# A searched instruction plan with two load queues and some operations free to go to either of two engines, for attention and two gated layers on one Trainium2 core

## The chip, the cores and the metric

The kernel runs on one core of one Trainium2 chip. A core has five instruction queues that run side by side, each in its own order: PE (matrix products), DVE (vector work), ACT (activations, copies), POOL (vector work, slower) and SP (here it only issues DMAs). They wait for each other by semaphores. The metric is device time in microseconds (us) of one launch, lower is better. Before the change three runs gave 1077.69, 1081.61 and 1084.92 us, with a median of 1081.61 us.

## The reference, cut to what matters

```python
scores = scale * np.matmul(q, k.transpose(0, 1, 3, 2))          # q, k, v: (4, 8, 576, 64)
thresh = np.max(scores, axis=-1, keepdims=True) - tau
scores = np.where(scores >= thresh, scores, -1000000000.0)
attn = np.exp(scores - np.max(scores, axis=-1, keepdims=True))
attn = attn / (np.sum(attn, axis=-1, keepdims=True) + 1e-09)
x = np.matmul(attn, v)                                           # then to (2304, 512)
h = x @ moe_w_in                                                 # (512, 2048)
x = (h * np.clip(h + 3.0, 0.0, 6.0) / 6.0) @ moe_w_out           # (2048, 512)
h = x @ moe2_w_in
out = (h * (1.0 / (1.0 + np.exp(-1.702 * h)))) @ moe2_w_out
```

## The kernel before, in words

A matrix product in full precision is done as three products of a high and a low part of each operand (high x high, high x low, low x high). Much of the work of DVE, ACT and POOL is making such parts: a copy to the reduced type gives the high part, a subtraction the low part.

The work has three stages. In **attention** a unit is one pair of heads of one batch (16 units). For each of its nine tiles PE makes scores (tile `ps`, L566; L582 and L598 in the first four units), DVE takes the row maximum (`nm`, L614) and the threshold (`th`, L615), ACT the exponential (`e`, L616), DVE cuts and sums it (L617). Then `e` is normalised (L630 on POOL, later units), transposed (PE L668 and ACT L671, or DVE and a DMA through memory), multiplied with v (L709, L726), and its result `xr` is split into `xh` and `xl`. Between the units of attention the **first half of the first gated layer** runs as its inputs come (`moe_a`: hidden products L785, gate L796 and L797, high part on ACT, low part on POOL, output products L805). Then come the rest of the first layer (`moe_b`) and the **second layer** (`moe2`, hidden products L942 by a scheme with fewer products, output products L805). Weights come as 64-bit numbers and are decoded in `decode` (ACT L419, DVE L420 to L422, POOL adds through the helper at L369) and split. The helpers at L366 (ACT copy) and L369 (two-operand operation on DVE or POOL) stand for many operations, so a row of theirs is told by its tiles.

Nothing of the order is written out by hand. Every operation is an entry of a plan with an engine, a cost in ns and dependencies. `settle` simulates the plan, ranks operations by how late they may run, then disturbs the ranks with nine fixed seeds (`KICKS`), ranks again after each, and the last simulated start times give the program's order on every queue. `PORT` names the operations of DVE and POOL that the plan doesn't let run at the same time. `fill` puts stand-in matmuls (L1105, of constants, their result unused) where the plan has PE idle for over about half a microsecond and a result bank is free. So a stand-in marks a gap that the plan itself sees:

```python
count = int((s - t) / 450 if s < 12000 else (s - t - 300) / 216)
if count > 0:
```

All DMAs are issued by SP, in plan order, and an SP wait holds back the issues behind it. For the first units, the two heads' k come in two loads of 64 rows (L526), their q in five (L525 and L530).

## Time and profile before

| | |
|---|---|
| median of three runs | 1081.61 us |
| the profiled execution | 1084.38 us |
| its span, first to last instruction | 1082.5 us |
| PE busy | 1057.6 us (98%) |
| DVE busy | 733.3 us (68%) |
| ACT busy | 634.3 us (59%) |
| POOL busy | 516.2 us (48%) |
| data moved | 141.78 MB, 131 GB/s on average |

Busy time is the union of an engine's instructions. The span is split below into six stretches: the start (0 to 24 us), the rest of the first units (to 62, where the first hidden product of the gated layer starts), the next units (to 135), attention with the first half of the first layer (to 433), the rest of the first layer (to 690), and the second layer (to the end).

### The profile page before, as it was taken

Reading aid. Unit: us, or ns where it says so; the run is one execution under the profiler, and the core shown is the slowest. Engines: PE = TensorE matmul, PEld = TensorE weight load, DVE = VectorE, ACT = ScalarE, POOL = GpSimd, SP = SyncE. Lnnn points to the kernel's source line nnn. Section 1 sums busy time; section 2 is a strip of 40 time slices with the busy share of each in tenths; the row PEclk is TensorE's granted clock in tenths of the full one; section 3 lists DMA queues with packets and bytes.
Section 4 is the critical chain, followed back from the end, with each engine's and each line's share of the span. In section 5 each row is a group of like instructions: output and inputs, shape, how many; then the busy total and the mean of one; then the engine's idle time right before and its main releaser. Section 6 shows DMA issues by size and latency. Waiting matters only on the chain.

```text
span 1082.5 us, 20424 instructions
## 1 busy us (share of the span) xinstructions
PE 1057.6 (98%) x7498; PEld 961.9 (89%) x7498; DVE 733.3 (68%) x1541; ACT 634.3 (59%) x1272; POOL 516.2 (48%) x597
## 2 busy tenths in 40 slices
PE   8899899999999999999999999999999999999998
PEld 6677788799889988999999999889988889989888
DVE  6898977777767772677874333888786684563634
ACT  4798777576657664766453234665565565444433
POOL 3688978776777662755474225432322333001000
PEclk9999999999999999999999999999999999999999
DMA  6334375655465435445744112426553542312202
GB/s 198 120 115 140 115 207 148 183 146 155 139 186 146 149 102 168 130 146 175 215 139 135 59 58 60 158 63 207 182 176 106 166 158 87 117 54 65 93 1 74
DMA packets 87172, 141.78 MB, mean 131 GB/s; under 512 B 8608, under 2 KB 51232, under 8 KB 85536
## 3 DMA queue, kind: packets, MB, share of 16 engines
q1 hardware_dynamic: 87072, 140.48, 43.0%
q8 instruction: 59, 0.97, 0.4%
q14 instruction: 41, 0.34, 0.1%
HBM read 97.32 MB, written 43.12 MB: 130 GB/s over the span
## 4 chain that ended last, share of the span: by engine, by line
PE 77%; DMA 8%; DVE 5%; POOL 3%; ACT 2%; SPq 2%; issue 2%; DVEq 0%; POOLq 0%; ACTq 0%
PE py L805 25%; PE pm L942 15%; PE pm L785 15%; PE pm L805 7%; PE pm L726 6%; PE ps L566 5%; PE pm L668 3%; DMA qk<-in_q_dram 1%; DMA kept<-wmstg 1%; DMA et<-turned 1%; DMA wrawstg<-in_w1i_dram 1%; POOL wmstg L369 1%; DMA yc<-ypd 1%; DMA wrawstg<-in_w1o_dram 1%; DVE nm L614 1%
## 5 line engine op out<-in xcount | busy, mean ns | idle before, releaser
L805 PE MATMUL py<-g,outhring 128*128 128x512 f32 (+2 forms) x1152 | 289.2, 338 | 6.1 <-DVE g L369 1.9
L805 PEld LDWEIGHTS py<-g,outhring 128*128 128x128 f32 x1152 | 193.5, 188 | 25.4 <-DVE g L369 4.3
L805 PE MATMUL py<-g,outlring 128*128 128x512 f32 (+2 forms) x576 | 193.4, 336 | 0.0
L785 PE MATMUL pm<-xh,inhring 128*128 128x256 f32 (+1 forms) x512 | 153.2, 299 | 0.2
L785 PE MATMUL pm<-xl,inhring 128*128 128x256 f32 (+1 forms) x512 | 150.8, 295 | 0.0
L785 PE MATMUL pm<-xh,inlring 128*128 128x256 f32 (+1 forms) x512 | 150.8, 294 | 0.0
L942 PE MATMUL pm<-outhring,inhring 128*128 128x256 f32 x512 | 144.7, 283 | 1.8 <-DVE c L369 1.5
L942 PE MATMUL pm<-outlring,inhring 128*128 128x256 f32 x512 | 143.9, 281 | 0.1
L942 PE MATMUL pm<-outhring,inlring 128*128 128x256 f32 x512 | 143.6, 281 | 0.0
L614 DVE TENSOR_REDUCE nm<-ps 128x1 f32<-128x576 f32 x144 | 106.8, 751 | 33.2 <-PE ps L566 27.3
L369 POOL TENSOR_TENSOR g<-t,g 128x256 fp32r<-128x256 f32 (+1 forms) x104 | 87.9, 850 | 78.6 <-ACT g L366 69.8
L617 DVE SCALAR_TENSOR_TENSOR e<-ps,th,e 128x576 f32<-128x576 f32 x128 | 102.4, 811 | 23.6 <-ACT e L616 22.6
L805 PEld LDWEIGHTS py<-g,outlring 128*128 128x128 f32 x576 | 108.2, 188 | 9.9
L369 POOL TENSOR_TENSOR wmstg<-wmstg,wrstg 128x512 uint32<-128x512 uint32 x48 | 66.2, 1380 | 103.6 <-DVE wmstg L422 67.8
L616 ACT ACTIVATE e<-ps,nm 128x576 f32<-128x576 f32 x128 | 93.2, 740 | 33.8 <-DVE nm L614 26.2
L796 ACT ACTIVATE t<-pm,half 128x256 f32<-128x256 f32 (+1 forms) x128 | 63.9, 499 | 77.8 <-PE pm L785 69.2
L805 PE MATMUL pm<-g,outhring 128*128 128x256 f32 (+1 forms) x512 | 108.1, 302 | 0.5 <-ACT et L671 0.5
L369 POOL TENSOR_TENSOR g<-tc,g 128x512 fp32r<-128x512 f32 x24 | 32.4, 1351 | 157.5 <-ACT g L366 135.8
L797 DVE SCALAR_TENSOR_TENSOR t<-t,pm 128x256 f32<-128x256 f32 (+1 forms) x128 | 57.4, 449 | 69.2 <-ACT t L796 66.3
L942 PEld LDWEIGHTS pm<-outhring,inhring 128*128 128x128 f32 x512 | 96.9, 189 | 6.0 <-DVE c L369 2.0
L942 PEld LDWEIGHTS pm<-outlring,inhring 128*128 128x128 f32 x512 | 96.9, 189 | 3.1 <-DVE outlring L369 0.3
L785 PEld LDWEIGHTS pm<-xh,inhring 128*128 128x128 f32 x512 | 96.6, 189 | 1.2 <-PE pm L1105 0.7
(114 smaller groups left out, 2428.7 us busy)
## 6 DMA issues: line engine op xcount, KB each, us to landing
turned<-tr SPq DMA_DIRECT2D x12, 1024.0 KB, 3.9
et<-turned SPq DMA_DIRECT2D x48, 256.0 KB, 6.0
wrawstg<-in_w1i_dram SPq DMA_DIRECT2D x16, 512.0 KB, 4.0
wrawstg<-in_w1o_dram SPq DMA_DIRECT2D x16, 512.0 KB, 3.9
wrawstg<-in_w2i_dram SPq DMA_DIRECT2D x16, 512.0 KB, 4.3
wrawstg<-in_w2o_dram SPq DMA_DIRECT2D x16, 512.0 KB, 4.1
qk<-in_k_dram SPq DMA_DIRECT2D x24, 288.0 KB, 3.8
qk<-in_q_dram SPq DMA_DIRECT2D x24, 288.0 KB, 3.6
```

Of the source, the lines that this page charges most:

```text
L369: return lambda: (nc.vector if eng == DVE else nc.gpsimd).tensor_tensor(out=o(), in0=a(), in1=b(), op=op)
L566: nc.tensor.matmul(ps.t[:, i, :SH], qss[hd].t[:, q0:q0 + P], w[hd].t[:, i * SH:(i + 1) * SH], start=a, stop=z)
L614: add(DVE, 665, K("R", s), "R", lambda: nc.vector.tensor_reduce(out=nm.t[:, c], in_=ps.t[:, :, :SH], op=ALU.max, axis=AX.XY, negate=True), ...
L616: add(ACT, 624, K("X", s), "X", lambda: nc.scalar.activation(out=ev(), in_=ps.t[:, :, :SH], func=ACTF.Exp, bias=nm.t[:, c]), [ps, (nm, s)] ...
L617: add(DVE, 729, K("M", s), "M", lambda: nc.vector.scalar_tensor_tensor(out=ev(), in0=ps.t[:, :, :SH], scalar=th.t[:, c], in1=ev(), op0=ALU ...
L668: nc.tensor.transpose(pt.t[:kn, o:o + P], e_of[s].t[:, keys(k)], id_b.t)
L726: nc.tensor.matmul(pv[p].t[64 * hd:64 * hd + 64, :CH[p][1]], v_(k, hd), x, start=k == 0, stop=k == 4)
L785: nc.tensor.matmul(ph.t[:, :n], a, v, start=(cc == 0 and i == 0), stop=(cc == KC - 1 and i == 2))
L796: add(ACT, 93 + act(n), K("RL"), "RL", lambda: nc.scalar.activation(out=tt_(), in_=pt(), func=ACTF.Relu, scale=1.0 / 6.0, bias=half_b.t), ...
L797: add(DVE, dve(n), K("GT"), "GT", lambda: nc.vector.scalar_tensor_tensor(out=tt_(), in0=tt_(), scalar=1.0, in1=pt(), op0=ALU.min, op1=ALU. ...
L805: nc.tensor.matmul(py.t[:, :n], a, v, start=(st and i == 0), stop=(sp and i == 2))
L942: nc.tensor.matmul(o.t[:, :n], u.t[:, ws], v.t[:, xv], start=(st and kk == 0 and i == 0), stop=(sp and kk == 1 and i == 2), skip_group_che ...
```

## The change

The plan's costs are nearer to some durations (decode on ACT 575 ns for 520, weight loads 1.4 times as long, POOL's two-operand work a little longer). The nine seeds become 28, and about 330 further steps (`SHAKES`) follow, each of which shifts the ranks in a small window; a negative number instead swaps one operation to its other engine. Operations that may swap have an `alt`: most splits (ACT to DVE, POOL to DVE and back), the normalisation (POOL to DVE), thresholds (DVE to ACT), the first step of decode (DVE to POOL), copies out of PE's banks (ACT to DVE). `tau` and the first half of the first q are issued by ACT; k of the first four units comes in one load of 128 rows.

```diff
-PORT = {DVE: {"W", "XHB", "XLB", "XD", "XLC", "GT2", "GL"}, POOL: {...}}
+PORT = {DVE: {"W", "XHB", "XLB", "XD", "XLC", "GT2", "GL", "qs", "N", "kl", "XL", "XH", "GH", "kh", "qh", "ql"}, POOL: {...}}
-KICKS = (9, 22, 44, 100, 235, 395, 771, 940, 4389)
+KICKS = (
+    1032833269, 966046151, -163, 557497160, -877, 57522857, 697246556, 315576823, 472954259, -947, 719353647, 1052280090, 511556057, 211244978, -5437, 720474978,
...
+SHAKES = (
+    584305649, -943, 243327645, 788971575, 33716921, 162258981, -1247, 1025097930, -949, 1049297085, 494265569, 331174672, -197, 382340551, 170708664, 94164452,
...
         for seed in KICKS:
-            self.order(kicked(key, length, seed))
-            key = self.latest()
+            if seed < 0:
+                op = self.ops[-seed]
+                (op.eng, op.cost, op.fn), op.alt = op.alt, (op.eng, op.cost, op.fn)
+                self.link()
+                key = self.latest()
+            else:
+                self.order(kicked(key, length, seed, kinds, len(names)))
+                key = self.latest()
             length = self.order(key)
+        ref = key
+        for seed in SHAKES:
+            if seed < 0:
+                op = self.ops[-seed]
+                (op.eng, op.cost, op.fn), op.alt = op.alt, (op.eng, op.cost, op.fn)
+            else:
+                key = kicked(key, length, seed, kinds, len(names), ref)
+        self.link()
+        self.order(key)
...
-    move(-30000, "tau", 4 * P, lambda: nc.sync.dma_start(out=tau_b.t, in_=tau), [], [tau_b])
+    move(-30000, "tau", 4 * P, lambda: nc.scalar.dma_start(out=tau_b.t, in_=tau), [], [tau_b], ACT)
...
-                move(K("ld"), "ldk", 256 * S, lambda r=r, h=2 * j + hd: nc.sync.dma_start(out=f32(khb.t)[r, :S], in_=k2[b, h, :64]), [], [(khb, hd)])
...
+                eng, q = (ACT, nc.scalar) if u + hd == 0 else (SP, nc.sync)
...
+            move(K("ld") - 8000 * (u == 0), "ldk", 512 * S * 1.4, lambda rows=rows: nc.sync.dma_start(out=f32(khb.t)[:, :S], in_=k2.rearrange("b h p s -> (b h p) s")[rows:rows + P]), [], [khb])
...
-            add(ACT, act(size), K("EH", at), "EH", lambda: nc.scalar.activation(out=dst(kn)[0], in_=dst(kn)[1](pt.t[:kn, :size]), func=ACTF.Copy), [pt], [(et, tag)])
+            add(ACT, act(size), K("EH", at), "EH", lambda: nc.scalar.activation(out=dst(kn)[0], in_=dst(kn)[1](pt.t[:kn, :size]), func=ACTF.Copy), [pt], [(et, tag)], (),
+                (DVE, dve(size), lambda: nc.vector.tensor_copy(out=dst(kn)[0], in_=dst(kn)[1](pt.t[:kn, :size]))))
```

What the swaps come to, counted from the two programs: 28 operations go from POOL to DVE (21 subtractions of two operands, 7 scalings), 33 from ACT to DVE (21 between buffers, 12 out of PE's banks), 11 scalings from DVE to POOL, 22 thresholds from DVE to ACT. PE's program has the same matmuls, but 31 stand-ins in 7 places in the place of 49 in 16: behind the first hidden product one is left where 19 stood. The rows of both programs at three places follow.

SP at the program's start, before (`g` holds q, `kqv` holds k, `wrawstg` the first raw weights):

```order
L381 DMA tau_106<-in_tau_dram 128x1
L525 DMA g_141<-in_q2_dram 64x256 x2
L526 DMA kqv_157<-in_k2_dram 64x576 x2
L525 DMA g_147<-in_q2_dram 64x256 x2
L526 DMA kqv_170<-in_k2_dram 64x576 x2
L382 DMA id_103<-in_ident_dram 128x128
L525 DMA g_151<-in_q2_dram 64x256 x2
L526 DMA kqv_175<-in_k2_dram 64x576 x2
L525 DMA g_155<-in_q2_dram 64x256 x2
L526 DMA kqv_181<-in_k2_dram 64x576 x2
L409 DMA wrawstg_244<-in_w1i_dram 128x4x256
```

SP at the same place now:

```order
L590 DMA g_140<-in_q2_dram 64x256
L592 DMA kqv_151<-in_k2_dram 128x576
L590 DMA g_148<-in_q2_dram 64x256 x2
L592 DMA kqv_168<-in_k2_dram 128x576
L444 DMA id_103<-in_ident_dram 128x128
L590 DMA g_154<-in_q2_dram 64x256
L592 DMA kqv_176<-in_k2_dram 128x576
L590 DMA g_154<-in_q2_dram 64x256
L590 DMA g_158<-in_q2_dram 64x256
L592 DMA kqv_184<-in_k2_dram 128x576
L590 DMA g_158<-in_q2_dram 64x256
L471 DMA wrawstg_224<-in_w1i_dram 128x4x256
```

The first weight load is the 19th issue before and the 13th now; the first k moves from the fourth and fifth issue to the second, and one q and `tau` stand on ACT's queue ahead of its table load.

DVE where the first weights are decoded, before (`wmstg` is the decoded tile, `nm`, `th` and `e` belong to score tiles):

```order
L617 SCALAR_TENSOR_TENSOR e_247,sm_221<-ps_233,th_213,e_247 128x576
L615 TENSOR_SCALAR th_213<-nm_210,nt_108 128x1
L617 SCALAR_TENSOR_TENSOR e_255,sm_221<-ps_241,th_213,e_255 128x576
L614 TENSOR_REDUCE nm_282<-ps_268 128x1
L420 TENSOR_SCALAR wmstg_280<-wmstg_280 128x512
L615 TENSOR_SCALAR th_293<-nm_282,nt_108 128x1
L624 RECIPROCAL rc_295<-sm_221 128x4
L421 TENSOR_SCALAR wmstg_280<-wmstg_280 128x512
```

and now:

```order
L690 SCALAR_TENSOR_TENSOR e_248,sm_220<-ps_234,th_214,e_248 128x576
L687 TENSOR_SCALAR th_214<-nm_209,nt_108 128x1
L690 SCALAR_TENSOR_TENSOR e_254,sm_220<-ps_240,th_214,e_254 128x576
L482 TENSOR_SCALAR wmstg_258<-wmstg_258 128x512
L484 TENSOR_SCALAR wmstg_258<-wmstg_258 128x512
L686 TENSOR_REDUCE nm_287<-ps_272 128x1
L485 SCALAR_TENSOR_TENSOR wmstg_258<-wrawstg_224,wmstg_258 128x512
L687 TENSOR_SCALAR th_303<-nm_287,nt_108 128x1
```

The decode steps L420 to L422 are L482 to L485 now; two of them stand ahead of the fifth tile's maximum, where one stood behind it.

PE at the first hidden product, before (`two` is the stand-ins' constant, `xh`, `xl` and `inhring`, `inlring` the parts of x and of the weights):

```order
L656 MATMUL pm_743<-id_103,bt_677 128x128 x2
L1105 MATMUL pm_754<-two_105 128x128 x2
L598 MATMUL ps_757<-kqv_157,kqv_160 128x288
L598 MATMUL ps_759<-kqv_157,kqv_160 128x288
L598 MATMUL ps_757<-kqv_157,kqv_160 128x288
L598 MATMUL ps_759<-kqv_157,kqv_160 128x288
L1105 MATMUL pm_779<-two_105 128x128 x2
L785 MATMUL pm_782<-xh_0_488,inhring1_369 128x256
L785 MATMUL pm_782<-xl_0_495,inhring1_369 128x256
```

and now:

```order
L732 MATMUL pm_731<-id_103,bt_666 128x128 x2
L1188 MATMUL pm_742<-two_105 128x128
L670 MATMUL ps_744<-kqv_151,kqv_162 128x288
L670 MATMUL ps_746<-kqv_151,kqv_162 128x288
L670 MATMUL ps_744<-kqv_151,kqv_162 128x288
L670 MATMUL ps_746<-kqv_151,kqv_162 128x288
L1188 MATMUL pm_777<-two_105 128x128 x10
L863 MATMUL pm_788<-xh_0_504,inhring1_336 128x256
L863 MATMUL pm_788<-xl_0_512,inhring1_336 128x256
```

Ten stand-ins stand directly ahead of the first hidden product (L863 now) where two stood, and one ahead of the scores where two stood.

## Rows read from the trace of the kernel before

**Rows 1.** Busy by stretch: length, PE, PEld, DVE, ACT, POOL us; clock, DMA share, GB/s

```profile
0.00:24.00 24.00, 19.84 (x108) 16.33 (x109) 15.98 (x46) 10.88 (x17) 7.26 (x27) 1.00 0.68 192
24.00:62.00 38.00, 34.33 (x222) 24.75 (x218) 32.79 (x80) 30.17 (x59) 23.16 (x27) 0.96 0.42 127
62.00:135.00 73.00, 68.92 (x512) 56.04 (x513) 66.77 (x159) 60.48 (x118) 64.18 (x77) 1.00 0.42 124
135.00:433.00 298.00, 296.15 (x2263) 263.63 (x2262) 209.67 (x521) 192.99 (x382) 207.03 (x288) 1.00 0.55 157
433.00:690.00 257.00, 254.43 (x1915) 253.50 (x1914) 155.96 (x297) 131.96 (x269) 132.50 (x120) 1.00 0.42 126
690.00:1082.50 392.50, 383.91 (x2490) 347.70 (x2488) 252.16 (x445) 207.83 (x432) 82.05 (x61) 1.00 0.35 112
sum 1082.50, PE 1057.58 PEld 961.94 DVE 733.33 ACT 634.32 POOL 516.17; mean PE 176.26 PEld 160.32 DVE 122.22 ACT 105.72 POOL 86.03
```

**Rows 2.** The same view of the stand-ins' line L1105 alone (PE, PEld)

```profile
0.00:24.00 24.00, 8.25 (x48) 7.86 (x48) 1.00 0.68 192
...
135.00:433.00 298.00, 3.10 (x22) 2.88 (x22) 1.00 0.55 157
...
690.00:1082.50 392.50, 2.58 (x16) 2.48 (x16) 1.00 0.35 112
```

**Rows 3.** PE's waits: who waited for whom, us in total, times, longest

```profile
PE ps L566 <- DVE e L617: 2.9, 5, 1.4
...
PE py L805 <- DVE yc L369: 1.6, 1, 1.6
```

**Rows 4.** Timeline of the start: start, duration, engine, instruction, [idle before <- releaser]

```profile
2.38 1.24 SPq L526 DMA_DIRECT2D kqv<-in_k_dram  x2
...
5.06 0.63 POOL L503 MEMSET et<- 64x640 f32 x1
...
6.01 2.48 PE L582 MATMUL ps<-kqv,g 128*128 128x288 f32 x8
...
11.83 1.14 SPq L409 DMA_DIRECT2D wrawstg<-in_w1i_dram  x2
...
17.80 0.43 DVE L420 TENSOR_SCALAR wmstg<-wmstg 128x512 f32<-128x512 f32 x1 [1.38 <-ACT wmstg L419]
...
20.30 0.97 PE L582 MATMUL ps<-kqv,g 128*128 128x288 f32 x3 [1.72 <-DVE th L615]
```

**Rows 5.** DMA issues by line: how many, KB each, median us from issue to landing

```profile
qk<-in_k_dram SPq DMA_DIRECT2D x24, 288.0 KB, 3.8
...
kqv<-in_k_dram SPq DMA_DIRECT2D x8, 144.0 KB, 2.9
```

**Rows 6.** PE by stretch from 30 to 37.4 us, columns as Rows 1

```profile
30.00:34.00 4.00, 1.62 (x11) 0.99 0.48 142
34.00:37.40 3.40, 3.40 (x10) 0.51 0.11 39
```

**Rows 7.** Timeline at 515 us, at 814 us and at the end

```profile
515.72 1.49 DVE L369 TENSOR_TENSOR g<-t,g 128x256 fp32r<-128x256 f32 x1
...
517.27 0.39 PE L805 MATMUL py<-g,outhring 128*128 128x256 f32 x1 [1.00 <-DVE g L369]
...
814.07 0.66 ACT L419 ACTIVATE wmstg<-wrawstg 128x512 f32<-128x512 f32 x1 [3.07 <-DMA kept<-wmstg]
...
1079.05 0.28 PE L805 MATMUL py<-g,outlring 128*128 128x256 f32 x1
```

**Rows 8.** Groups by line, tiles and shape: busy us, mean ns, idle before

```profile
L369 POOL TENSOR_TENSOR kqv<-qk,kqv 128x576 fp32r<-128x576 f32 x24 | 34.8, 1450 | 12.9 <-PE pm L726 8.8 <-issue 3.6
...
L369 DVE TENSOR_TENSOR g<-t,g 128x256 fp32r<-128x256 f32 x8 | 7.5, 945 | 1.4 <-ACT g L366 1.4
...
L369 DVE TENSOR_TENSOR g<-tc,g 128x256 fp32r<-128x256 f32 x16 | 6.2, 421 | 0.8 <-ACT g L366 0.5
...
L527 DVE TENSOR_SCALAR g<-g,sc 128x512 f32<-128x512 f32 x4 | 2.0, 488 | 2.9 <-DMA g<-in_q_dram 2.0 <-POOL et L503 0.9
```

More of the change, by code (lines that the diff above doesn't have):

```diff
@@ L250, in fill, with kicked, draw @@
         return out
-def kicked(key, length, seed):
-    rng = random.Random(seed)
-    size, width = rng.choice((100.0, 300.0, 1000.0, 3000.0)), rng.choice((2e4, 6e4, 2e5, 2e6))
-    lo = rng.uniform(-length - width / 2, 0.0)
-    return [k + rng.gauss(0.0, size) if lo <= k < lo + width else k for k in key]
+def kicked(key, length, seed, kinds, count, ref=None):
+    def draw():
+        nonlocal seed
+        seed = (seed * 6364136223846793005 + 1442695040888963407) & 0xFFFFFFFFFFFFFFFF
+        return (seed >> 33) / 2147483648.0
+    for _ in range(4):
+        draw()
+    widths, odds = ((2e4, 6e4, 2e5, 2e6), 3) if ref is None else ((1e3, 4e3, 1.2e4, 4e4), 2)
+    size, width = (100.0, 300.0, 1000.0, 3000.0)[int(draw() * 4)], widths[int(draw() * 4)]
+    lo = draw() * (length + width / 2) - length - width / 2
+    noise, kind = int(draw() * 4) < odds, int(draw() * count)
+    shift = (draw() * 2 - 1) * size * 3
+    out = list(key)
+    for o, r in enumerate(ref or key):
+        if lo <= r < lo + width:
+            if noise:
+                out[o] += (draw() + draw() - 1) * 2 * size
+            elif kinds[o] == kind:
+                out[o] += shift
+    return out
 @with_exitstack
@@ L433, in of @@
             return ap[:, lo:hi]
-        add(ACT, 93 + 0.834 * n, time, "W", copy(lambda: h.t[:, :n], of), [src], [h])
-        add(eng, pool2(n) if eng == POOL else dve(n), time, "W", tt(eng, lambda: l.t[:, :n], of, lambda: f32(h.t)[:, :n], ALU.subtract), [src, h], [l])
+        add(ACT, 93 + 0.834 * n, time, "W", copy(lambda: h.t[:, :n], of), [src], [h], (), (DVE, 69 + 0.521 * n, lambda: nc.vector.tensor_copy(out=h.t[:, :n], in_=of())))
+        add(eng, pool2(n) if eng == POOL else dve(n), time, "W", tt(eng, lambda: l.t[:, :n], of, lambda: f32(h.t)[:, :n], ALU.subtract), [src, h], [l], (),
+            (POOL + DVE - eng, dve(n) if eng == POOL else pool2(n), tt(POOL + DVE - eng, lambda: l.t[:, :n], of, lambda: f32(h.t)[:, :n], ALU.subtract)))
         return parts
@@ L797, in gated, with low @@
         add(DVE, dve(n), K("GT"), "GT", lambda: nc.vector.scalar_tensor_tensor(out=tt_(), in0=tt_(), scalar=1.0, in1=pt(), op0=ALU.min, op1=ALU.mult), [ph], [t])
-        add(ACT, 42 + act(n), K("GH"), "GH", copy(lambda: g.t[:, :n], tt_), [t], [(g, 0)])
-        add(gl, dve(n) if gl == DVE else pool2(n), K("GL"), "GL", tt(gl, lambda: g.t[:, 320:320 + n], tt_, lambda: f32(g.t)[:, :n], ALU.subtract), [t, (g, 0)], [(g, 1)])
+        add(ACT, 42 + act(n), K("GH"), "GH", copy(lambda: g.t[:, :n], tt_), [t], [(g, 0)], (), (DVE, 69 + 0.521 * n, lambda: nc.vector.tensor_copy(out=g.t[:, :n], in_=tt_())))
+        costs = {DVE: dve(n), POOL: pool2(n)}
+        def low(eng):
+            return tt(eng, lambda: g.t[:, 320:320 + n], tt_, lambda: f32(g.t)[:, :n], ALU.subtract)
+        add(gl, costs[gl], K("GL"), "GL", low(gl), [t, (g, 0)], [(g, 1)], (), (DVE + POOL - gl, costs[DVE + POOL - gl], low(DVE + POOL - gl)))
         return g
```

80 lines of the change are left out of this document (49 added, 31 removed), and 21 rows, old and new, of the table SHAKES.

## Prediction

> **What bounds the kernel now.** I read the page's busy shares first, then busy time by stretch, then the stand-ins' line, then PE's waits, and last the timelines where PE waits. PE is busy 1057.58 of 1082.5 us, and no other engine over 733 [rows 1], so only what PE waits for, or does for nothing, can be won. The reader sees in the six stretches how PE's idle time is spread, length less busy: 4.16, 3.67, 4.08, 1.85, 2.57 and 8.59 us, 24.9 in all [rows 1]. To that come the stand-ins, which count as busy but compute nothing: 8.25, 3.10 and 2.58 us in the first, fourth and sixth stretch [rows 2], 13.9 together (each stand-in leaves two records). So 38.8 us is the pot, and some of it can't be had: 6.0 us pass before the first scores [rows 4], and 3.2 us between PE's last matmul (1079.05 plus 0.28) and the end at 1082.5 [rows 7]. The waits are many and short; the largest pairs are 2.9 and 1.6 us [rows 3]. So this change can't give 10%, and it is a question of how much of some 30 us a better order gets.
>
> **The change part by part.** The matmuls that compute are the same, so PE's floor doesn't move.
>
> *The swaps as load.* POOL loses 28 operations of at most 1.45 us (its longest moved kind), 41 us at most, of 516. DVE gets 61; at 0.945 us each, its slow row, they are 58 us, and it would stand at 791 of 1082 without counting what it gives away [rows 1, 8]. No engine becomes the bound by its total; what matters is who stands in front of whom.
>
> *A. Start, 0 to 24 us: -2.9.* Now the first scores need two k loads, the second issued by 3.62 us, and come at 6.01 [rows 4]. One k load of 128 rows is issued second on SP; `tau` and one q no longer stand ahead of it, so at some 0.5 each (an issue of k takes 0.62, half of 1.24) it starts at about 1.3 where the first k started at 2.38. A load of its size lands after 3.8 us, one of half its size after 2.9 [rows 4, 5]. That makes 5.1, a gain of up to 0.9. But half of the first q is scaled on POOL now, behind clears that ended at 5.06 and one at 5.69 [rows 4]; with some 0.5 us for the scaling (0.488 for twice the size on DVE [rows 8]) and a semaphore the first tile can also be as late as 5.9. I take -0.5. Two of DVE's four q scalings leave its queue between the first tiles: 2 x 0.488 = -1.0 [rows 8]. And DVE stood 1.38 us before the first decode step because the weights had not landed, with a threshold behind it for which PE waited 1.72 [rows 4]. The first weight load is issued after 12 others on SP where it was 18: at 0.62 each about 3.7 us earlier than 11.83. The step still stands before the fifth tile, so if the load were not earlier the stall would stay; I take -1.4. Ends: 0 and -4.5.
>
> On the two half loads a page of the Trainium skill has a rule: DMA: Bandwidth & Descriptors, "Rules for kernel authors", says that two transfers to disjoint halves of the partitions aren't worth it and one over 128 partitions is to be used. The median landings, 2.9 for the half and 3.8 for the whole, agree. By the rule spreading loads over SP and ACT saves issue time only, which would make the ACT queue worth one or two issues of 0.62, no more than the sum has.
>
> *B. 24 to 62 us: -0.4.* Between 30 and 34 us PE was busy 1.62 of 4.00, and then for 3.4 us its granted clock was 0.51, the lower level of 1.2 GHz: 2.4 idle and 1.7 lost to the clock [rows 6]. With DVE's queue a little shorter and thresholds on ACT I take half of 4.1, -2.0. Against it 11 stand-ins stand before the first hidden product where four stood; at 3.10 us for 22 records, 0.28 for each pair, seven more are +2.0, and a few tenths of waits around the old ones go (-0.4). Units that are earlier wait here for weights or `xl`, so what A wins is partly given back. Ends: +2.0 and -2.5.
>
> *C. 62 to 135: -2.4.* Idle 4.08; the main pair is the score buffer waiting for DVE's cut `e` [rows 3]. DVE is busy 67 of 73 us here, POOL 64 [rows 1], so this is where relief counts: thresholds go to ACT, low parts leave POOL. I take 0.6 of it. Ends: 0 and -4.1.
>
> *D. 135 to 433: -3.2.* Ten of eleven stand-ins go (10/11 of 3.10 = 2.8), since the plan no longer has those gaps; of the 1.85 idle I take a quarter. Ends: 0 and -5.0.
>
> *E. 433 to 690: -1.3.* Two waits make up the 2.57: PE's buffer for a partial sum that was late by a DMA (1.6) and a low part on DVE that took 1.49 us for some 0.42 (1.00) [rows 3, 7, 8]. The plan saw neither (no stand-in is there). The first may come again, as the loads still follow weight loads on one queue. Half. Ends: +1.6 and -2.6.
>
> *F. 690 to the end: -5.3.* All stand-ins go: -2.58. Idle less the tail is 5.4; half of it comes from what the plan doesn't know, such as ACT standing 3.07 us behind a store before it can reuse a buffer [rows 7], so -2.7. Ends: 0 and -8.0.
>
> The sum is 15.5 us. The profiled execution took 1084.4 us (span 1082.5 and 1.9 around it), so it would be 1068.9. It stood 2.8 above the median of the runs shown, so in their terms **1066 us**, 1.4% faster.
>
> **The rivals.**
>
> *The plan is nearly right.* Then nearly all planned and unplanned waits go: the low ends add to 26.7 us, 1055 us. For it: from 135 us on, only one planned gap is left, and the costs are nearer. Against it: several of the biggest waits now have no stand-in before them, so the plan didn't see them.
>
> *The waits only move.* A tighter order has less slack for what the plan doesn't know; each gap that is planned away comes back as an unplanned one, as at 814 us. Then A's 2.9, half of the stand-ins in D and F (2.7) and nothing else remains: 5.6 less 1.6 in B, 4.0, so 1078 us, which can't be told from before. For it speaks E: DMA and low-part delays are not in the plan.
>
> *Slower: collisions of DVE with POOL.* A subtraction of 256 columns for `g` took 0.945 us on average in one group of eight and 0.421 in another of sixteen [rows 8]; the one at 515.72 took 1.49 and PE waited 1.00 [rows 7]. The swaps give DVE 49 more operations between buffers (28 from POOL, 21 from ACT). If each that collides costs PE 1.00, 16 eat up the forecast and at 27 the kernel is 1% slower, some 1093 us. Against it: the changed plan puts the moved kinds into `PORT`, and it takes 16 such waits where the pair in these rows is one.
>
> The Trainium skill speaks against these swaps: SBUF — State Buffer, "Who interferes with whom", says that only the port pair shared by DVE and GpSimd contends, and that it is an exclusive lock under which the loser stands still. The 1.49 us row agrees; by that rule every subtraction moved to DVE may stand still for a whole POOL operation.
>
> **How the numbers follow.** The likeliest case, about half of the pot, has 0.58, with 1058 to 1074 as its own range; nearly everything gone 0.18; waits only moved 0.18; collisions 0.06. About 1% is what a measurement of this kernel can tell from no change: faster means under 1070.8, slower over 1092.4. Of the likeliest case 0.48 lies under 1070.8 and 0.10 above, so faster is 0.48 + 0.18 = 0.66, the same 0.10 + 0.18 = 0.28, slower 0.06. The range leaves out the collisions, the lowest third of the second case and the upper third of the third, 0.18 in all: 1051 to 1079.
>
> **What would show it.** A: first scores between 5.0 and 5.9 us, no DVE wait at L482, no wait of PE for a threshold near 20 us. B: the granted clock stays at 1.00 from 30 to 40 us; the ten stand-ins are followed by the hidden product with a wait of a few tenths at most. C: PE idle under 2 us from there on for the next units. D and F: no stand-ins but one, and idle time that did not grow by what they took (5.4 us); if it did, the waits only moved. E: no wait of PE for `yc`. Collisions: the mean of moved subtractions over 0.9 us, and PE waits with a low part on DVE as the releaser. The prediction is wrong if PE's idle time without start and tail stays above 13 us, or if the clock falls to the lower level where the stand-ins are gone.

## The result and the profile after

The changed kernel took 1067.82 us (median of four runs, 1066.82 to 1069.15), the one before 1082.55 beside it (four runs, 1077.69 to 1084.92). The ratio is 0.987, with a 95% interval of 0.9834 to 0.9907: 1.3% faster, where 1066 us had been forecast and 1051 to 1079 as the range. The profiled execution took 1067.58 us with a span of 1065.8.

Busy time by stretch, columns as in [rows 1]:

```profile
0.00:24.00 24.00, 20.42 (x108) 15.98 (x110) 17.23 (x47) 12.72 (x21) 11.80 (x31) 1.00 0.80 227
24.00:60.00 36.00, 34.85 (x235) 25.86 (x232) 33.71 (x85) 30.64 (x58) 26.93 (x31) 1.00 0.42 125
60.00:135.00 75.00, 71.72 (x542) 59.45 (x540) 69.59 (x160) 58.26 (x117) 60.78 (x74) 1.00 0.43 130
135.00:433.00 298.00, 296.73 (x2287) 265.58 (x2286) 226.77 (x545) 194.31 (x393) 202.06 (x279) 1.00 0.55 158
433.00:690.00 257.00, 254.17 (x1894) 251.50 (x1893) 160.09 (x309) 126.19 (x255) 127.00 (x112) 1.00 0.42 125
690.00:1065.80 375.80, 371.23 (x2409) 337.65 (x2407) 242.40 (x432) 202.60 (x419) 85.60 (x58) 1.00 0.36 114
```

The same view of the stand-ins alone (L1188 now; PE, PEld), where [rows 2] had 8.25, 3.10 and 2.58 us in the first, fourth and sixth stretch:

```profile
0.00:24.00 24.00, 6.73 (x38) 6.34 (x38) 1.00 0.80 227
24.00:60.00 36.00, 2.88 (x22) 2.61 (x22) 1.00 0.42 125
...
135.00:433.00 298.00, 0.39 (x2) 0.30 (x2) 1.00 0.55 158
...
690.00:1065.80 375.80, 0.00 (x0) 0.00 (x0) 1.00 0.36 114
```

PE's idle time (length less busy) fell from 24.9 to 16.7 us, the stand-ins from 16.31 us (all their records) to 10.00. That is 14.5 us, and most of the span's 16.7. The granted clock is 1.00 in every stretch; before, it stood at 0.51 for 3.4 us from 34 us on [rows 6], which at half the speed is an estimated 1.7 us lost. That fall doesn't come in every execution: of 38 further runs of the kernel before, 27 have a mean granted clock of 0.996 to 0.998 and take 1081.6 us on average, the other 11 (0.999 and 1.000) 1079.0. All four runs of the changed kernel stand at 1.00. POOL and ACT are a little less busy, DVE more (749.8 for 733.3).

PE's waits in the whole run (who waited for whom, us in total, times, longest):

```profile
PE py L888 <- DVE g L431: 1.6, 5, 0.5
PE ps L654 <- DVE e L690: 1.5, 3, 0.7
PE pm L732 <- DVE th L687: 1.4, 1, 1.4
...
PE py L888 <- DVE yc L431: 0.6, 2, 0.4
...
PE ps L638 <- DVE e L690: 0.3, 1, 0.3
```

The lines have moved: L566, L582 and L598 are L638, L654 and L670 now. So the two pairs of [rows 3] answer to the last line here (`e`, 2.9 us before) and to the one above it (`yc`, 1.6 before). The second line belongs to the scores of the first units, and there `e` costs PE what it cost before (1.6 us in two waits of L582). No wait over 1.4 us is left.

The timeline of the start (start, duration, engine, instruction, idle before and its releaser), to be read beside [rows 4]:

```profile
1.33 0.86 ACTq L443 DMA_DIRECT2D tau<-in_tau_dram  x1
1.34 0.57 SPq L592 DMA_DIRECT2D kqv<-in_k_dram  x1
...
4.90 0.15 DVE L446 TENSOR_SCALAR big<-tau 128x1 f32<-128x1 f32 x1 [3.57 <-DMA tau<-in_tau_dram]
...
5.62 2.69 PE L654 MATMUL ps<-kqv,g 128*128 128x288 f32 x6 [0.46 <-DVE g L594]
...
7.66 0.59 SPq L471 DMA_DIRECT2D wrawstg<-in_w1i_dram  x1
...
15.24 0.42 DVE L482 TENSOR_SCALAR wmstg<-wmstg 128x512 f32<-128x512 f32 x1
...
19.39 1.21 PE L654 MATMUL ps<-kqv,g 128*128 128x288 f32 x4 [0.59 <-DVE e L690]
```

The first weight load is issued at 7.66 us (11.83 before), and the first decode step on DVE comes at 15.24 without a wait (17.80 before, with 1.38). The first scores come 0.39 us earlier. They could have come sooner: k was issued at 1.34, but all scaling needs `tau`, and that stands behind a q on ACT's queue and landed only at 4.90.

Where the time went is read best from four places of the program, the starts of PE instructions in each timeline. The table has them for every kernel of this study (us; the last column is the span of the profiled execution):

| kernel | first hidden product | last attention x v | first product of layer 2 | span |
|---|---|---|---|---|
| before | 61.91 | 426.75 | 687.28 | 1082.5 |
| after | 57.90 | 416.90 | 677.34 | 1065.8 |
| a_home | 58.36 | 419.77 | 677.19 | 1065.0 |
| a_home_late | 58.27 | 417.90 | 674.77 | 1062.9 |
| a_kicks_only | 57.74 | 422.45 | 680.74 | 1067.4 |
| a_no_search | 57.44 | 437.88 | 695.40 | 1091.7 |
| a_no_swaps | 58.09 | 431.90 | 693.90 | 1088.3 |
| c_old_kicks | 61.46 | 443.09 | 701.29 | 1095.4 |
| a_old_loads | 62.72 | 423.19 | 682.16 | 1070.9 |
| b_new_loads | 58.02 | 421.95 | 680.55 | 1073.4 |
| b_no_late_standins | 61.56 | 426.25 | 685.21 | 1075.8 |
| a_no_standins | 55.73 | 418.61 | 677.83 | 1067.0 |
| a_tau_first | 59.17 | 418.81 | 678.19 | 1066.6 |
| a_tau_warm | 57.21 | 418.62 | 678.34 | 1067.2 |

Stage by stage, before to after: -4.0 us up to the first hidden product, -5.8 from there to the last attention product, -0.1 in the rest of the first layer, -6.8 in the second layer.

Each kernel has one trace, and the table shows how far one trace can be trusted. `after`, `a_old_loads`, `a_no_standins`, `a_tau_first` and `a_tau_warm` have the same order and the same swaps in the rest of the first layer, and take 258.97 to 260.44 us there. `before` and `b_new_loads` have the same order and stand-ins in the second layer, and take 395.22 and 392.85. So a difference of under some 2 us in a stage of two traces says little by itself.

### The profile page after: what moved, and what is told of

It is laid out like the page before. It is cut to its first block, busy times and chain, and to the rows that moved or that the text cites. A ratio compares the mean times of both kernels' runs of the same rounds, so it can differ in the third digit from the quotient of the medians.

```text
span 1065.8 us, 20332 instructions
## 1 busy us (share of the span) xinstructions
PE 1049.1 (98%) x7462; PEld 956.0 (90%) x7462; DVE 749.8 (70%) x1570; ACT 624.7 (59%) x1261; POOL 514.2 (48%) x580
## 4 chain that ended last, share of the span: by engine, by line
PE 80%; DVE 9%; DMA 3%; ACT 3%; POOL 2%; issue 2%; SPq 1%; ACTq 0%; POOLq 0%; DVEq 0%
PE py L888 24%; PE pm L863 15%; PE pm L1025 15%; PE pm L888 7%; PE pm L803 6%; PE ps L638 6%; PE pm L744 4%; PE pm L786 1%; PE ps L670 1%; DVE outlring L431 1%; DVE nm L686 1%; DVE wmstg L485 1%; DVE g L431 1%; DVE wmstg L484 1%; DVE e L690 1%
## 5 line engine op out<-in xcount | busy, mean ns | idle before, releaser
L888 PEld LDWEIGHTS py<-g,outhring 128*128 128x128 f32 x1152 | 190.4, 188 | 17.6 <-DVE g L431 3.2
L863 PE MATMUL pm<-xh,inhring 128*128 128x256 f32 (+1 forms) x512 | 153.6, 300 | 0.6 <-DVE t L875 0.3
L863 PE MATMUL pm<-xl,inhring 128*128 128x256 f32 (+1 forms) x512 | 150.8, 295 | 0.0
L863 PE MATMUL pm<-xh,inlring 128*128 128x256 f32 (+1 forms) x512 | 150.8, 294 | 0.0
L431 POOL TENSOR_TENSOR g<-t,g 128x256 fp32r<-128x256 f32 (+1 forms) x100 | 83.2, 838 | 82.4 <-ACT g L428 75.3
L431 POOL TENSOR_TENSOR wmstg<-wmstg,wrstg 128x512 uint32<-128x512 uint32 x48 | 71.1, 1482 | 103.7 <-DVE wmstg L485 82.2
L863 PEld LDWEIGHTS pm<-xh,inhring 128*128 128x128 f32 x512 | 96.6, 189 | 2.5 <-DVE t L875 0.6
```

The costliest lines, as they stand in the source:

```text
L431: return lambda: (nc.vector if eng == DVE else nc.gpsimd).tensor_tensor(out=o(), in0=a(), in1=b(), op=op)
L863: nc.tensor.matmul(ph.t[:, :n], a, v, start=(cc == 0 and i == 0), stop=(cc == KC - 1 and i == 2))
L888: nc.tensor.matmul(py.t[:, :n], a, v, start=(st and i == 0), stop=(sp and i == 2))
```

## Experiments

The change has four parts that can be pulled apart: the loads, the costs, the search (28 kicks, some 330 local steps), and the swaps, which are both work moved between engines and steps of the search. My theory was that the order itself gives the gain, by fewer planned gaps and fewer short waits; the rivals, that the swapped work gives it, that the loads do, or that the stand-ins alone do. Totals are medians, ratios are against the kernel before, run beside each.

### The swapped work put back, the order kept

Each operation keeps its place in the found order, but runs on the engine it had before any swap (at the end of `settle`; `home` is the first engine's function):

```diff
+        for o in self.ops:
+            o.fn = o.home
```

> The changed kernel's program order on every place, but each of the swapped operations (28 from POOL to DVE, 33 from ACT to DVE, 11 from DVE to POOL, 22 from DVE to ACT) runs on its old engine, at the same place among the others. Theory order (the searched order closes PE's gaps, the swaps are part of what it was searched with): time goes back in part, 1071 to 1078 us, with PE's new waits behind POOL or ACT in attention, before 135 us. Theory swaps (the relief of POOL and ACT is the gain): back to 1080 or above. Theory order alone (the swaps give nothing): within 2 us of 1067.8. If DVE and POOL collide more because of the swaps, it would even be faster than 1067.8.

Measured: 1067.02 us, ratio 0.9874 (0.9844 to 0.9904). DVE is at 728.8 us of busy time, ACT at 631.4, POOL at 522.9, near the kernel before, and the time is that of the changed kernel. So in sum the moved work is worth nothing that the intervals show; the gain lies in what stayed, the order and the loads.

### The search taken away

`KICKS` and `SHAKES` are empty, so the plan is only ranked three times; loads and costs stay new:

```diff
-KICKS = (1032833269, ...)
+KICKS = ()
-SHAKES = (584305649, ...)
+SHAKES = ()
```

> The changed kernel with neither kicks nor shakes: the ranks of the first four simulations set the order, no swap is made. 74 stand-ins in 12 places. Theory order: slower than the kernel before, 1085 to 1100 us, by about what the further stand-ins and their gaps take. Rival (the search as a whole moves little): below 1080.

Measured: 1090.43 us, ratio 1.0093 (1.0065 to 1.0122). The stand-ins (L1162 there) by stretch show what the plan without a search sees:

```profile
135.00:433.00 298.00, 6.59 (x46) 6.00 (x46) 0.99 0.55 153
...
690.00:1100.00 410.00, 5.01 (x42) 4.86 (x42) 1.00 0.35 111
```

There is 6.59 us in the fourth stretch and 5.01 in the sixth, where the changed kernel has 0.39 and 0. The last attention product is 21 us later than in the changed kernel, the second layer 7.8 longer. The stand-ins are the smaller part of those 21. From 60 to 135 us the plan has none, and all engines together show (columns as in [rows 1]):

```profile
60.00:135.00 75.00, 65.19 (x467) 51.69 (x467) 63.32 (x145) 57.60 (x111) 59.67 (x72) 0.95 0.38 118
```

PE idles 9.81 us there (3.28 in the changed kernel) and the granted clock is 0.95 in the mean: most of this loss the plan didn't see.

### The kicks alone

`SHAKES = ()`, so the 28 kicks with their ten swaps stay and the local steps go.

> The changed kernel without the some 330 steps of SHAKES: only the 28 kicks with their few swaps set the order. Its PE program has 52 stand-ins in 11 places, about as many as the kernel before (49 in 16). Theory order (local moves close the gaps that the plan sees): most of the gain goes, 1076 to 1082 us. Theory loads and costs (the new loads and the corrected costs carry it, the local moves fit the plan and not the chip): within 4 us of 1067.8.

Measured: 1068.84 us, ratio 0.9884 (0.9862 to 0.9907). The kicks carry nearly all of it; the local steps are worth about 1 us here, which the intervals can't tell from none. By the stages of the table the two don't do the same, though. With the kicks alone the second layer is the shortest of all (386.66 us, 388.46 in the changed kernel) and the stretch from the first hidden product to the last attention product no shorter than before (364.71 for 364.84); the local steps win 5.7 us there and give some 4 back behind it. This kernel has 52 stand-ins, more than the 49 of before, in 11 places:

```profile
0.00:24.00 24.00, 7.82 (x46) 7.43 (x46) 1.00 0.81 233
24.00:60.00 36.00, 4.39 (x34) 4.11 (x34) 1.00 0.40 121
...
135.00:433.00 298.00, 2.72 (x20) 2.50 (x20) 1.00 0.54 156
...
```

So the number of stand-ins, on which I had leant, doesn't measure an order: with 15.53 us of them in place of 10.00 the total is the same within the intervals.

### The seeds without the swaps

All kicks and local steps are made, but a negative number does nothing, and the order is simulated anew:

```diff
             if seed < 0:
-                op = self.ops[-seed]
-                (op.eng, op.cost, op.fn), op.alt = op.alt, (op.eng, op.cost, op.fn)
+                pass
```

> The changed kernel with every shift of ranks but without any swap, so that each operation is planned on its old engine with its old cost: the order is simulated anew and differs from the changed kernel's almost everywhere. 90 stand-ins in 19 places. Since the changed order with all operations back on their old engines took no longer, the swaps as work are worth nothing; what this run asks is whether the ranks alone hold an order. Theory: ranks were tuned with the swaps in place, each small misfit in the plan is left as a gap, 1078 to 1090 us. Rival (the ranks carry the order): 1066 to 1070 us.

Measured: 1089.78 us, ratio 1.0079 (1.0051 to 1.0106), with 96 stand-ins (192 records in the trace, where 90 had been expected). This seems to contradict the first experiment, and doesn't: there the order was kept, here the ranks that the seeds give meet another plan. The seeds fit only the plan for which they were picked.

### The old seeds on the new costs and loads

Costs, `PORT` and loads as changed; seeds and the way of disturbing ranks as before, no swaps, no local steps:

```diff
-KICKS = (1032833269, ...)
+KICKS = (9, 22, 44, 100, 235, 395, 771, 940, 4389)
-SHAKES = (584305649, ...)
+SHAKES = ()
```

> The changed kernel with the old search: the nine old seeds and the old way of disturbing ranks, no swaps, no shakes, but the new costs and the new loads. Its PE program has 87 stand-ins in 23 places. Theory search (the new kicks with their swaps carry most of the gain, the costs alone none): 1078 to 1088 us, so near the kernel before or above it. Rival costs (a plan nearer to the chip is what gives the gain, whichever seeds): 1067 to 1073 us.

Measured: 1097.21 us, ratio 1.0145 (1.0121 to 1.0168). With these seeds the nearer costs give nothing; the nine had been picked for the old plan. What the costs are worth to seeds that are picked for them isn't shown: no run here searches as long on the old costs, or takes the seeds away from the old plan.

### The loads, undone and alone

After with `tau` and the first q back on SP and each k in two loads of 64 rows, the order kept:

```diff
-    move(-30000, "tau", 4 * P, lambda: nc.scalar.dma_start(out=tau_b.t, in_=tau), [], [tau_b], ACT)
+    move(-30000, "tau", 4 * P, lambda: nc.sync.dma_start(out=tau_b.t, in_=tau), [], [tau_b], ACT)
...
-                eng, q = (ACT, nc.scalar) if u + hd == 0 else (SP, nc.sync)
+                eng, q = (ACT, nc.sync) if u + hd == 0 else (SP, nc.sync)
...
```

> The changed kernel's order with the loads as before: tau and the first q on SP at the same places, each of the first four k in two loads of 64 rows. SP then has 17 issues ahead of the first weights where it has 12. Theory loads (A was forecast as 2.9 us, of it 1.4 for earlier weights and 0.5 for earlier scores): 1 to 3 us above 1067.8, the first scores at 6.0 us or later, and again a wait of DVE for the first weights before 20 us. Rival (DVE's chain of the first tiles covers the loads): within 0.7 us.

Measured: 1070.74 us, ratio 0.9906 (0.9882 to 0.9931): 2.9 us over the changed kernel by the medians, 3.9 by the ratios, whose intervals meet. The old stall is back, and in the profiled execution the clock falls (timeline of DVE, behind a copy on ACT that waited 3.15 us for the load; then busy time by stretch):

```profile
17.66 0.43 DVE L482 TENSOR_SCALAR wmstg<-wmstg 128x512 f32<-128x512 f32 x1 [2.85 <-ACT wmstg L481]
```

```profile
18.00:22.00 4.00, 0.93 (x6) 0.74 (x6) 3.50 (x7) 2.98 (x6) 1.29 (x1) 1.00 0.96 271
22.00:28.80 6.80, 5.80 (x16) 3.81 (x18) 5.07 (x14) 3.81 (x8) 3.23 (x4) 0.51 0.86 251
```

The first hidden product is 4.8 us later than in the changed kernel, but this execution is the slowest of the four (1072.70 us, mean clock 0.996). The run that stands at 1.00 took 1070.47, still over all four of the changed kernel, so the fall isn't needed for the loss. The other side, before with nothing but these loads (`tau` and one q on ACT, `tau` first there; whole k loads):

```diff
-                move(K("ld"), "ldk", 256 * S, lambda r=r, ...: nc.sync.dma_start(out=f32(khb.t)[r, :S], in_=k2[b, h, :64]), [], [(khb, hd)])
+                move(K("ld"), "ldk", 256 * S, lambda hd=hd, rows=...: None if hd else nc.sync.dma_start(out=f32(khb.t)[:, :S], in_=k2.rearrange("b h p s -> (b h p) s")[rows:rows + P]), [], [(khb, hd)])
```

> The kernel before, every operation at its place, with the new loads alone: k of the first four units in one load of 128 rows at the place of its first half, tau and the first half of the first q on ACT's queue (tau first). Theory loads (the old loads cost the changed kernel 2.9 us): 2 to 3.5 us faster than the kernel before, DVE no longer waits for the first weights near 17.8 us, and the first hidden product comes 2 to 4 us earlier. Rival (the old order waits elsewhere for what the loads give): within 1 us of before.

Measured: 1076.18 us, ratio 0.9956 (0.9933 to 0.9979), which is 4.8 us by the ratio (2.3 to 7.3 by its interval). The decode step comes at 16.44 us without a wait, the first hidden product at 58.02, as early as in the changed kernel, and the clock doesn't fall at 34 us. So the loads alone explain the start, and leave some two thirds of the whole gain to the order (half to five sixths by that interval).

### The late stand-ins taken from before

No stand-ins behind the first hidden product (`H`); they compute nothing that is used:

```diff
-                count = int((s - t) / 450 if s < 12000 else (s - t - 300) / 216)
+                count = 0 if late else int((s - t) / 450 if s < 12000 else (s - t - 300) / 216)
+                late |= op.name == "H"
```

> The kernel before, with the 19 stand-in matmuls behind the first hidden product left out, all else in the same order. Theory cover (a stand-in fills a gap in which PE would wait anyway): within 1.5 us of the kernel before, and PE's idle time grows by about what the stand-ins took, 5.7 us. Theory cost (the stand-ins hold up ready work, so that their removal is 5.7 us of the gain by itself): 1076 to 1078 us. Theory clock: the granted clock falls to the lower level at one of these places and the time is above before by 2 us or more.

Measured: 1077.46 us, ratio 0.9975 (0.9958 to 0.9992). The 5.7 us of [rows 2] that went are worth 2.7 by the ratio (0.9 to 4.5 by its interval). Some was idle time that came back, and in the profiled execution the clock fell a second time (three of the ten runs stand at a mean clock of 1.00):

```profile
118.80:122.20 3.40, 3.40 (x14) 2.98 (x16) 1.66 (x4) 1.19 (x3) 3.23 (x5) 0.50 0.00 0
```

### No stand-ins in the changed kernel

`count = 0` in `fill`.

> The changed kernel without any stand-in matmul. Theory cover with the clock: without them PE is idle for much of the first 20 us, the granted clock there is at the lower level, the first scores take twice their time, and the total is 1 to 5 us above 1067.8. Theory that they cost time: the ten ahead of the first hidden product took 2.5 us, of which at most some 0.3 lay on the path, so at most 0.5 us below 1067.8.

Measured: 1069.51 us, ratio 0.9901 (0.987 to 0.9931). The first hidden product comes 2.2 us earlier, which is what the ten stand-ins before it took. It is given back at once: PE then stands 2.05 us, and the scores behind it (L670) start at 58.39 us, where they start at 58.36 in the changed kernel. So these ten fill time in which PE would have waited. The clock comes later, behind a gate for which both kernels wait, 1.34 us here (until 70.91) and 1.36 in the changed one (until 70.83); only here it falls:

```profile
66.00:70.90 4.90, 3.57 (x23) 2.57 (x22) 3.79 (x10) 3.18 (x8) 4.17 (x4) 1.00 0.35 109
70.90:74.30 3.40, 3.39 (x14) 1.59 (x16) 3.40 (x9) 3.14 (x6) 2.27 (x3) 0.50 0.00 0
```

The clock stands at half for 3.4 us, and the last attention product is 1.7 us later than in the changed kernel, about what such a fall costs. The total is no better. So the stand-ins that are left cost nothing that the total shows; that this fall comes of their absence is not shown by one trace.

### `tau` ahead of q

After with the order of the two issues on ACT's queue changed (the functions of the entries `ldq` and `tau` change places).

> The changed kernel, but on ACT's queue tau is issued ahead of the first q instead of behind it. In the profile of the changed kernel the first vector operation that reads tau starts at 4.90 us where it was 2.77 before, and the first scores wait for a scaling of q that needs it. Theory tau (the late tau sets the first scores): the first scores come at about 5.0 to 5.3 us instead of 5.62, and the total falls by 0.3 to 0.8 us. Rival (k's landing at about 5 us sets them anyway, and DVE's softmax chain behind it is the bound to 20 us): the first scores move by under 0.2 us and the total by under 0.3.

Measured: 1067.85 us, ratio 0.9881 (0.9853 to 0.9909): the same. The first scores come at 5.08 us in place of 5.62, and it is lost by 20 us (timeline; L601 scales q, L434 is the helper, L657 makes scores there):

```profile
16.92 1.30 POOL L434 TENSOR_TENSOR wmstg<-wmstg,wrawstg 128x512 uint32<-128x512 uint32 x1 [1.77 <-ACT et L750]
16.95 1.48 DVE L601 TENSOR_SCALAR kqv<-kqv,sc 128x384 f32<-128x384 f32 x1
...
19.98 1.37 PE L657 MATMUL ps<-kqv,g 128*128 128x288 f32 x3 [1.90 <-DVE e L693]
20.10 0.41 DVE L601 TENSOR_SCALAR kqv<-kqv,sc 128x384 f32<-128x384 f32 x1
```

A scaling on DVE that starts 0.03 us behind a POOL addition takes 1.48 us, where the same one alone takes 0.41; the cut behind it is late, PE idles 1.90, and then the clock falls, to 0.50 from 20.4 to 23.8 us. That is the profiled execution; three of the five runs stand at a mean clock of 1.00 and take 1066.03 to 1067.87, so the fall is not what ate the gain. To tell the clock from the collision I gave this kernel three times the stand-ins at 18 us, and 3 for 10 before the first hidden product:

```diff
+                count = 3 * count if 12000 <= s < 25000 else min(count, 3) if s > 25000 else count
```

> The changed kernel with tau ahead of the first q on ACT's queue, three times the stand-ins before the scores near 18 us (9 for 3) and three instead of ten ahead of the first hidden product. With tau first alone the granted clock fell to the lower level from 20.4 to 23.8 us, behind 1.9 us in which PE was idle, and the total did not move. Theory clock (the fall ate the gain): the clock stays at 1.00 past 20 us and the total is 1065 to 1067 us. Rival collision (DVE's 1.48 us scaling behind a POOL operation, not the clock, ate it): the fall is gone but the total stays within 0.7 us of 1067.8.

Measured: 1067.79 us, ratio 0.987 (0.9851 to 0.9888). The clock stays at 1.00, the collision is shorter (the scaling takes 1.10, PE idles 0.46 behind it), and the first hidden product comes at 57.21. Yet the total doesn't move: the last attention product is at 418.62, the same as with `tau` first alone. So half a microsecond at the start, with or without the clock, doesn't show in the total of this order.

### The late swaps alone put back

The first layer's second half had given nothing, and the profiles of after and of the kernel with all swaps put back differed just there (2.83 and 1.50 us of idle time from 433 to 690). So the 71 swaps up to the last attention product stay, and the 23 behind it run on their old engines, 19 of them ahead of the second layer's first product. Of those 19, 16 had gone to DVE:

```diff
+        for o in self.ops:
+            if self.start[o.n] > 401000:
+                o.fn = o.home
```

> The changed kernel's order and swaps up to the last product of attention weights and v (planned at 401 us); the 23 swapped operations planned behind it, 19 of them before the second layer's first product, run on the engine that they had before the swap. In the profiles of the changed kernel and of the one with all swaps undone in place, PE idles 2.83 and 1.50 us between 433 and 690 us. If the swaps there cause the difference, this kernel idles 1.5 to 1.9 us in the stretch from the last attention product to the second layer's first product, its waits for DVE g there fall from 1.1 us to some 0.4, and the total is 1.0 to 1.5 us shorter than the changed kernel's: 1066.3 to 1066.8 us. If the difference is chance, or comes from how the earlier swaps shift the queues, it idles 2.6 to 3.0 us there and takes 1067.5 to 1068.

Measured: 1064.92 us (1064.84 to 1066.80), ratio 0.9853 (0.9835 to 0.9871), the lowest median of all. It is 2.9 us under the changed kernel by the medians and 1.8 by the ratios, whose intervals overlap, so the total alone doesn't settle it. The stage shows it better: from the last attention product to the second layer this kernel takes 256.87 us and the one with all swaps put back 257.42, where the five kernels with the changed order and these swaps take 258.97 to 260.44. So the late swaps cost 1.6 to 3.6 us there. PE's waits around this stage, first of the changed kernel, then of this one (its last line lies in the second layer already):

```profile
PE py L888 <- DVE g L431: 1.1, 3, 0.5
PE py L888 <- DVE yc L431: 0.6, 2, 0.4
PE py L888 <- ACT g L428: 0.5, 2, 0.3
PE pm L863 <- ACT ys L428: 0.2, 1, 0.2
```

```profile
PE pm L866 <- ACT ys L431: 0.5, 1, 0.5
PE pm L1028 <- DVE outlring L434: 0.4, 1, 0.4
```

The waits for `g` and `yc` are gone. Two of them stand in all five kernels with the late swaps and in neither without, and a moved operation stands ahead of both. The first, in the changed kernel and then in this one:

```profile
487.31 0.42 DVE L498 CAST inhring<-wmstg 128x512 fp32r<-128x512 f32 x1
487.81 1.41 POOL L431 TENSOR_TENSOR inlring<-wmstg,inhring 128x512 fp32r<-128x512 f32 x1 [1.04 <-DVE inhring L498]
487.98 1.59 DVE L431 TENSOR_TENSOR g<-t,g 128x320 fp32r<-128x320 f32 x1
490.23 0.41 DVE L431 TENSOR_TENSOR yc<-py,yc 128x256 f32<-128x256 f32 x1
490.78 0.53 PE L888 MATMUL py<-g,outhring 128*128 128x320 f32 x2 [0.39 <-DVE yc L431]
```

```profile
487.67 0.49 DVE L434 TENSOR_TENSOR g<-t,g 128x320 fp32r<-128x320 f32 x1
489.59 0.42 DVE L434 TENSOR_TENSOR yc<-py,yc 128x256 f32<-128x256 f32 x1
```

The high part `inhring` had moved from ACT to DVE. It holds up the low part `g`, which then runs beside a POOL subtraction and takes 1.59 us for 0.49, and the sum `yc` comes 0.64 later. Ahead of the other (`g` at 503.54 us, 0.41 idle) DVE stood 1.06 us for a decode step that had moved to POOL. The largest wait of the fence is not of this kind:

```profile
480.24 0.48 DVE L482 TENSOR_SCALAR wmstg<-wmstg 128x512 f32<-128x512 f32 x1 [1.24 <-ACT wmstg L481]
480.56 0.39 PE L888 MATMUL py<-g,outhring 128*128 128x256 f32 x1 [0.27 <-ACT g L428]
480.98 0.41 DVE L431 TENSOR_TENSOR g<-t,g 128x256 fp32r<-128x256 f32 x1
481.44 0.38 PE L888 MATMUL py<-g,outhring 128*128 128x256 f32 x1 [0.49 <-DVE g L431]
```

This low part and the decode steps ahead of it run on DVE in both kernels. DVE stood behind a copy on ACT that had waited 1.23 us for a load of weights, and with all swaps put back PE waits here too (0.44). Three more of the fence's eight waits, from 517 to 521 us, stand in this trace alone.

The run was expected to save 1.0 to 1.5 us and saved more. One reason is that the idle column shows less than a wait costs: products of this line follow each other at 0.12 us where nothing waits, and the one at 481.44 starts 0.88 behind the one at 480.56, so 0.76 are lost where 0.49 are shown as idle.

## Why the prediction was right, and where not

**The total** came out as forecast, 1067.82 for 1066, by the case called likeliest, about half of the pot. The sum was 15.5 us for the profiled execution, and 16.8 were measured (1084.38 to 1067.58); between the medians it is 14.7. That it fits so closely is in part luck: terms erred both ways, the pot left out 2.38 us of stand-ins in the second stretch (16.31 in all, not 13.9), and the trace of before has a slow second layer, as said above.

| terms | forecast | measured |
|---|---|---|
| A and B, to the first hidden product | -3.3 | -4.0 |
| C and D, to the last attention product | -5.6 | -5.8 |
| E, to the second layer | -1.3 | -0.1 |
| F, the second layer | -5.3 | -6.8 |

**A** was right in its place and parts: first scores between 5.0 and 5.9 (5.62), no wait of DVE at L482, the first weight load 4.2 us earlier for 3.7 forecast. What I missed is `tau`: I let it start early on ACT's queue without asking when it lands. It landed 3.5 us after its issue behind a q, and DVE stood 3.57 us. The loads without the search gave 4.8 us of the total, and undoing them cost 2.9; that this is the very value forecast for A is chance, with intervals of some 2 us to either side.

**B** was right: PE is busy 3.44 of 4.00 us from 30 to 34 us (1.62 before, [rows 6]), the clock stays at 1.00, and the ten stand-ins are followed by the hidden product without a wait:

```profile
30.00:34.00 4.00, 3.44 (x18) 2.10 (x20) 3.96 (x13) 3.68 (x7) 2.64 (x4) 1.00 0.17 41
...
55.35 2.50 PE L1188 MATMUL pm<-two 128*128 128x128 f32 x20
57.90 0.39 PE L863 MATMUL pm<-xh,inhring 128*128 128x256 f32 x1
```

Their 2.50 us was put down as a loss of 2.0. Taking them away gave 2.2 at that place and nothing in the end, since PE stands 2.05 us right behind it then.

**C and D** came out in sum, and by luck. In D stand-ins fell by 2.7 and idle time by 0.6, both as forecast. C did not do what was said of it: from 60 to 135 us PE still idles 3.28 us (4.14 before), over the mark of 2. The waits of the later scores for `e` went from this stretch, and two others came, the 1.4 for a threshold shown further up and a second one as long (first before, then after):

```profile
PE ps L566 <- DVE e L617: 2.2, 3, 1.4
```

```profile
PE pm L786 <- DVE t L875: 1.4, 1, 1.4
```

From the first hidden product to the last attention product idle time fell by 1.3 us and stand-ins by 2.1. The other 2.4 of the 5.8 is time that counts as busy on PE, which the sum had put at nothing ("PE's floor doesn't move"). And the account by which stand-ins that go are time won was too simple: in the kernel before, 5.7 us of them were worth 2.7, and the kernel with the kicks alone has more stand-ins than before and is 1.2% faster.

**E** is the step that failed. I took half of two waits of 1.6 and 1.00 us as won (-1.3), and the stage took as long as before (-0.1). Those two went, and eight shorter ones came. Those of them that recur in every kernel with the late swaps and in none without stand behind moved operations, of which 16 of 19 in this stage had gone to DVE. Without these swaps the stage is 3.7 us shorter than in the trace of before, more than the 2.6 of the low end. So the rival of collisions on DVE was real in this one stage, as a queue and a collision in turn; it cost 1.6 to 3.6 us, not 27.

**F** was right in kind and, by this pair of traces, too small: stand-ins went from 2.58 to 0, and idle time without the tail fell from 5.4 us to 1.1 (4.57 of the stretch, less 3.5 between PE's last matmul and the end), where half had been forecast. Against the trace with the new loads alone, whose second layer has the old order, the gain is 4.4 us, so the size of F stays between 4.4 and 6.8.

**The swaps as load** were costed at nothing, which held for the sum of all (1067.02 without them). The late ones lose what was said under E. Whether the 71 early ones win it back isn't shown: from the first hidden product to the last attention product it takes 361.41 us without them, and 359.00 to 361.41 in the five kernels that have them and whose clock didn't fall there. The means of the moved kind show no general slowing: for `g`, subtractions of 256 columns on DVE took 562 ns, where [rows 8] had 945, and those of 320 columns 666, where they had taken 588.

**The marks** that I had set: PE's idle time behind the first stretch and without the tail is 9.6 us (17.5 before), under the 13 at which the forecast would have been wrong, and the clock didn't fall where stand-ins went. Two marks were missed, the 2 us of C and the `yc` of E (0.6 us in two waits). The rival of waits that only move (1078) is excluded by the interval for the total; it held in part of C and in E. The plan nearly right (1055) isn't reached, nor by the best kernel here, 1064.92.

Open is in part why the kernels with `tau` first are no sooner; at the last attention product both stand at 418.6 to 418.8, 1.7 to 1.9 us behind the changed kernel. With `tau` first alone 1.3 of that is there at the first hidden product already, behind the collision and the fall of the clock. With the stand-ins that keep the clock up that product comes 0.7 early, but PE then stands 1.07 us for the cut `e` on DVE, and the scores behind it start at 58.90 us, 0.5 behind the changed kernel. Where the other 1.2 go isn't shown; with one trace each, it may be the changed kernel's trace that is early. Open, too, are what the nearer costs are worth to a search, and what besides waits and stand-ins the found order shortens.

## What to carry to other kernels

Ask of a searched order first what it does to the waits behind which PE stands, stage by stage between fixed places of the program; counts of planned gaps and engine totals said little. An order found by a search fits only the plan it was found for: seeds without their swaps, or old seeds on better costs, made the kernel 0.8% to 1.5% slower than before. Where an operation may go to either of two engines, put it back where the move holds up what the bound engine waits for; here that alone gave 1.6 to 3.6 us in one stage.

## What the runs showed of the hardware that was not expected

The clock's falls that are shown above look alike: the granted clock goes from 1.00 to 0.50 or 0.51, the lower level of 1.2 GHz, for 3.4 us or for 6.8, and what stands ahead is a stretch in which PE idled: busy 3.57 of 4.90 us with one gap of 1.3 in the kernel without stand-ins, 0.93 of 4.00 ahead of the 6.8 us with the old loads. But such a stretch doesn't settle it: in the changed kernel PE was busy 3.54 us of the same 4.90, with a gap of 1.36, and the clock didn't fall. Where PE was busy 3.44 of 4.00, in the changed kernel too, it didn't fall, nor where it was busy 2.54 of 4.00, from 30 to 34 us in the kernel with the new loads alone. Nor does a kernel's clock fall in each of its runs: with `tau` first three of five stand at a mean of 1.00. At half the speed a fall of 3.4 us costs an estimated 1.7, more than the gap of 1.3 in the kernel without stand-ins.

A one-input scaling of 128 x 384 numbers on DVE took 1.48 us beside a POOL addition of 1.30 and 0.41 alone. The Trainium skill says in SBUF — State Buffer, "Who interferes with whom", that `tensor_scalar` too can take the port pair shared with GpSimd and then one of the two stands still for the whole of the other's instruction. The trace agrees: 0.41 and most of 1.30 make the 1.48. I had weighed this rule for subtractions only.

A load of 0.5 KB, `tau`, took 3.5 us from its issue on ACT's queue, behind a q, to its landing, nearly as long as the loads of 288 KB for k (3.9 in the median). Issued first on the same queue, in the kernel before with the new loads, it took 2.1.
